# Dealing the first loads to three queues, and storing the last unit plainly: one change at both ends of a fused attention and Fourier-mix kernel

## The chip, the cores and the metric

The kernel runs on one core of a Trainium2 chip. A time is the device time of one launch in microseconds (us). The kernel before took 2325.61 us, the median of three runs (2323.56, 2325.61, 2325.95). A separate execution was recorded by the hardware profiler; its own time was 2316.28 us.

## The reference

All tensors are float32. The first half is talking-heads attention with 8 batches, 12 heads, 448 rows and head size 64; the second half is a Fourier mix followed by a feed-forward block.

```python
scores = (1 / sqrt(64)) * q @ k.T                       # per batch b and head h
scores = einsum('bhij,hg->bgij', scores, w_pre)         # mix heads before the softmax
attn = softmax(scores)                                  # over the last axis
attn = einsum('bhij,hg->bgij', attn, w_post)            # mix heads after it
x = (attn @ v), heads side by side                      # (8, 448, 768)
u = x + real(fft(fft(x, axis=1), axis=2))
un = (u - mean(u)) / sqrt(var(u) + 1e-6)
out = u + relu(un @ w_ch1) @ w_ch2                      # 768 -> 3072 -> 768
```

## The kernel before

The kernel has two phases. `mix_phase` does the attention and the Fourier mix; `ffn_phase` does the feed-forward block. The change touches the first 60 us of the one and the last 30 us of the other.

**The attention pipeline.** A batch has eight blocks of rows (`BLOCKS`), and a block has 2 or 3 *steps*, 23 in a batch, 184 in all. The data pass through these stages:

- `emit_load_qk` loads the rows of one head pair of q or k into a tile `raw`. A tile takes four DMAs (`y` is the half of the partitions, `x` the head), each of 112 KB. A batch has six such tiles, so 24 DMAs. `emit_load_v` loads v, six DMAs of 224 KB a batch.
- `emit_xpose` transposes a raw tile on TensorE (7 transposes, L598) and copies it out of PSUM in two parts, one on ScalarE and one on VectorE (`ENG`), into `qT` or `kT`.
- `emit_qk(n, xx)` computes the scores of block `n` for four heads (16 matmuls, L624) and copies them in two pieces into the score tile `Sb` (copies of every kind are on L487, the line of the helper `copy`). `ENG["QK"]` is "aa": both copies are on ScalarE. There are two `Sb` tiles, so the copies of block n wait until block n-2 has been read.
- `emit_gather(T)` rearranges the scores of step T, so that all heads of some rows lie on neighbouring partitions: four DMAs of 105 KB from `Sb` to a tile `Kr` (L641), on the queue of SyncE (SP).
- `emit_premix(T)` mixes heads (L652), `emit_max` takes row maxima on VectorE (L659), `emit_exp` exponentiates on ScalarE (L666), `emit_scale` normalises on GpSimd (POOL, L676), `emit_postmix` mixes heads again (L686), `emit_turn` transposes (L699).
- `emit_av` multiplies by v (L716); Fourier stages follow further on.

`emit_load_mix` loads the two small mixing matrices and a mask, seven small DMAs.

**The order** is written by hand. The main loop counts a step number `s` upward from the first entry. In each `s`, the gather is that of step s+5, the premix, maximum, exponential and scale are those of step s+2, and the postmix and turn are those of step s. All other work stands in four lists, filled by `due(kind, at, fn)`, and is issued when `s` reaches `at`. TensorE, VectorE, ScalarE and GpSimd keep exactly that order. A DMA issued from ScalarE or GpSimd therefore also stands in that engine's order: while the issue waits, what comes after it on the engine waits as well.

For the first batch all q and k loads are at -40 and in the order k, q for xx = 0, then 2, then 1 (`START`); of each pair of DMAs, `x = 0` is on SP and `x = 1` on ScalarE. The v loads follow on SP, then (-39) the seven small loads on SP. The six transposes are at -20 to -15, the scores of blocks 0 and 1 at -18 to -13 alternately. Block n from 2 on is at BLOCK_AT[n] - 8 + AT_QK[n][xx], which is -2, -1, 0 for block 2, then 1, 2, 2 for block 3 and 3, 4, 5 for block 4. The q and k of the second batch are loaded by GpSimd at the steps of `AT_L`: -4 and -3, -2 and -1, 0 and 1, 2 and 7, and so on.

**The last unit.** The feed-forward phase is cut into six chunks of the hidden dimension times seven tiles of 512 rows. A unit is one chunk of one tile: `first` computes the hidden part (L1208), `second2` the output part (L1330) as seven products j0, j3, j5, j6, j4, j1, j2, collected in tiles `od` by ScalarE (L1358) and VectorE (L1352). `both` adds one od tile to another (L1361). `out_` is a DMA from GpSimd that *adds* an od tile onto a quarter of the output tile in memory (L1364, 384 KB). `acc[t, r, d]` is the quarter with row half r and column half d. `on(s, ...)` places work at position s of the unit's 49 matmul pairs and their tail. In the last unit (`end`), two quarters, v12 and v22, are loaded from the output beforehand (`load`, L1338), the products are added to them on the chip, and they are written with two plain DMAs each, one on SP and one on ScalarE (`store`, L1368). The other two quarters are updated by four adding DMAs: j0 and j1 onto (0, 0), j3 and j6 onto (1, 0).

Of the kernel before, what the change touches and what calls it, by code (L numbers as in the profile page):

```python
# [17 lines left out]
B, NH, S, D = 8, 12, 448, 64  # L18
# [71 lines left out]
AT_L = ((-4, -3), (-2, -1), (0, 1), (2, 7), (10, 11), (12, 13))  # L90
AT_V = ((2, 3), (4, 5), (6, 7))
AT_QK = ((0, 2, 1), (0, 1, 2), (0, 1, 2), (1, 2, 2),
         (0, 1, 2), (0, 1, 2), (0, 1, 2), (0, 1, 2))
# [355 lines left out]
def mix_phase(ctx, tc, rest, ident, q, k, v, w_pre, w_post, u_scr, u_rev, wts, lead):  # L449
# [60 lines left out]
    def emit_load_mix():  # L510
        for t in dens:
            nc.gpsimd.memset(t[:, :, :], 1e-9)
        nc.gpsimd.memset(wrp[:, :, :], 0.0)
        nc.sync.dma_start(out=mk, in_=cn["mk"].ap())
        for x in range(2):
            for y in range(2):
                nc.sync.dma_start(
                    out=wrp[64 * x + 30 * y:64 * x + 30 * y + 30, 0, :],
                    in_=_ap(w_pre, 6 * y * NH, [[0, R], [NH, 6], [1, NH]]))
            nc.sync.dma_start(out=wrp[64 * x:64 * x + KR, 1, :],  # L520
                              in_=_ap(w_post, 0, [[0, R], [NH, NH], [1, NH]]))
# [33 lines left out]
    def emit_load_qk(b, xx, nm, y):  # L555

        src = q if nm == "q" else k
        if y == 0 and b == 0 and xx == START[-1]:

            if "raw" not in first:  # L560
                first["raw"] = ppv.tile([P, GT, 2 * S], F32, name="Pv", tag="Pv")
            batches[b]["raw" + nm, xx] = first["raw"][:, nm == "q"].rearrange(
                "p (c x d) -> p c x d", c=C7, x=2)
        elif y == 0:
            batches[b]["raw" + nm, xx] = praw.tile([P, C7, 2, D], F32, name="raw" + nm,
                                                   tag="raw")
        t = batches[b]["raw" + nm, xx]
        for x in range(2):
            eng = nc.gpsimd if b else (nc.sync, nc.scalar)[x]
            eng.dma_start(  # L570
                out=t[64 * y:64 * y + 64, :, x, :],
                in_=src[b, 6 * y + 2 * xx + x].rearrange("(p c) d -> p c d", c=C7))
        return True
# [10 lines left out]
    def emit_xpose(b, xx, nm):  # L584
# [6 lines left out]
        if nm == "q":  # L591
            nc.gpsimd.memset(t[:, :, 0:MG], 0.0)
            nc.gpsimd.memset(t[:, :, MG + S:WQ], 0.0)
        evs = []
# [15 lines left out]
    def emit_qk(n, xx):  # L610

        bk = blocks[n]
        st = batches[bk["b"]]
        if "Sb" not in bk:
            bk["Sb"] = psb.tile([P, 6, S], F32, name="Sb", tag="Sb")
# [3 lines left out]
        for y in range(2):  # L619
            for o in (64 * y, 64 * y + 32):  # L620
                lo = c0 + o - 64 + (0 if y else w)
                hi = min(lo + 32, c0 + w)
                for x in range(2):
# [4 lines left out]
                        start=True, stop=True)  # L628
        return [lambda x=x: copy(ENG["QK"][x], bk["Sb"][:n, 2 * xx + x, :],
                                 pss[x][:n, :S]) for x in range(2)]  # L630

    def emit_gather(T):

        Kr = pkr.tile([P, 2, S], F32, name="Kr", tag="Kr")
        n, j = at_step[T]
        Sb, rs = blocks[n]["Sb"], blocks[n]["rs"]
        row = _row(Sb)
        for z in range(2):
            for x in range(2):
                p0 = 64 - R * rs + 4 * j + 2 * z + x  # L640
                nc.sync.dma_start(  # L641
                    out=Kr[64 * x:64 * x + KR, z, :],
                    in_=_ap(Sb, p0 * row, [[rs * row, 2 * R], [S, 6], [1, S]]))
        steps[T]["Kr"] = Kr
# [242 lines left out]
    for b in range(B):  # L887
        f = b * GS
        at_t = [(a, nm, xx) for xx, at in enumerate(AT_T) for nm, a in zip("qk", at)]
        if b == 0:  # L890

            for i, xx in enumerate(START):
                for j, nm in enumerate("kq"):
                    for y in range(2):
                        due("none", -40, lambda xx=xx, nm=nm, y=y: emit_load_qk(0, xx, nm, y))
                    due("full", 2 * i + j - 20, lambda xx=xx, nm=nm: emit_xpose(0, xx, nm))
                for n in range(2):
                    due("QK", 2 * i + 2 + n - 20, lambda n=n, xx=xx: (emit_qk(n, xx), n))
            for pr in range(3):
                for y in range(2):  # L900
                    due("none", -40, lambda pr=pr, y=y: emit_load_v(0, pr, y))
        else:
            for at, (a, nm, xx) in zip(AT_L, sorted(at_t, key=lambda e: e[0])):
                for y in range(2):
                    due("none", f + at[y] - GS,
                        lambda b=b, xx=xx, nm=nm, y=y: emit_load_qk(b, xx, nm, y))
# [7 lines left out]
        for n in range(0 if b else 2, NBL):  # L914
            for xx in range(3):
                due("QK", f + BLOCK_AT[n] - 8 + AT_QK[n][xx],
                    lambda n=NBL * b + n, xx=xx: (emit_qk(n, xx), n))
# [24 lines left out]
    due("none", 0, lambda: wts.deal(0))  # L942
    due("none", -39, emit_load_mix)
    due("none", -3, emit_mix)
# [101 lines left out]
def ffn_phase(ctx, tc, rest, ident, u_scr, u_rev, wts, ub_scr, out, fold_rest,  # L1046
# [262 lines left out]
    def second2(n, st):  # L1309
# [76 lines left out]
        j0, j3, j5, j6, j4, j1, j2 = range(7)  # L1386
        v22, v12 = 7, 8
        pl = nc.gpsimd
# [5 lines left out]
        if end:  # L1394
            for v, r, d in ((v12, 0, 1), (v22, 1, 1)):
                on(0, load, v, r, d)
            on(24, out_, j0, 0, 0)
            on(27, out_, j3, 1, 0)
            for s, *o in ((33, vec, j5, j0), (34, pl, v12, j5), (41, vec, j6, j5),
                          (41, pl, v22, j6), (51.5, vec, v12, j4), (59, vec, v22, j4)):  # L1400
                on(s, both, *o)
            on(42, out_, j6, 1, 0)
            on(51.5, out_, j1, 0, 0)
            on(58, store, v12, 0, 1)
# [143 lines left out]
```

## Time and profile before

| | |
|---|---|
| median of three runs | 2325.61 us |
| profiled execution, its own time | 2316.28 us |
| its span, first to last instruction | 2314.3 us |
| TensorE busy | 2250.9 us, 97% of the span |
| VectorE, ScalarE, GpSimd busy | 1717.0, 1170.1, 1280.7 us |
| TensorE idle in the first 70 us | 24.3 us |
| last matmul to end of the span | about 11.6 us |

The profile names an instruction by its engine, its source line and the tiles it writes and reads ("Kr<-Sb"). "PEld" is the weight load, "SPq" or "ACTq" the queue of an engine that issues DMAs. In lists of instructions the first number is the start, the second the length, both in us, and the bracket at the end is the idle time before it and what ended that. In tables by stretch of time, each engine has its busy time and its count of instructions, and the last two columns are the mean busy share of the 16 DMA engines and what they moved.

### The profile page before, as it was taken

The numbers are of one execution on the slowest core, as the hardware profiler recorded it, in microseconds if no ns is written. First come the engines' busy times: TensorE is split into PE (matmuls) and PEld (weight loads), VectorE is DVE, ScalarE is ACT, GpSimd is POOL, SyncE is SP. The second block draws the span as 40 slices with busy tenths as digits, with TensorE's granted clock in tenths as the row PEclk, the third lists the DMA queues.
The fourth block names the chain that finished last, engine by engine and source line by source line (L and its number), as shares of the span: only waits on it lengthen the run. The fifth ranks groups of instructions, "written<-read, shape, count | busy, mean of one in ns | idle before, by whom it ended". The sixth has DMA issues, their size and how long they took to land.

```text
span 2314.3 us, 60776 instructions
## 1 busy us (share of the span) xinstructions
PE 2250.9 (97%) x22894; PEld 1737.6 (75%) x22894; DVE 1717.0 (74%) x3626; ACT 1170.1 (51%) x3336; POOL 1280.7 (55%) x1786
## 2 busy tenths in 40 slices
PE   5999999999999999999999999999999999999997
PEld 2545555555555577676899999999999999999997
DVE  2878888888878757777777787878778877765544
ACT  3776767666676632221345444444444445434433
POOL 3587868778787542221555454556555655453334
PEclk9999999999999999999999999999999999999999
DMA  7565665656656375668777887878787987796564
GB/s 164 160 185 163 190 175 163 193 160 190 181 175 196 133 260 190 209 200 290 216 171 192 227 228 187 220 182 247 207 190 186 278 193 174 186 257 124 133 144 75
DMA packets 232176, 439.44 MB, mean 190 GB/s; under 512 B 39624, under 2 KB 154336, under 8 KB 231886
## 3 DMA queue, kind: packets, MB, share of 16 engines
q1 hardware_dynamic: 157902, 302.97, 38.2%
q0 software_dynamic: 68128, 130.82, 29.9%
q8 instruction: 183, 3.00, 0.6%
q10 hardware_dynamic: 5856, 1.77, 0.4%
q14 instruction: 107, 0.88, 0.1%
HBM read 212.76 MB, written 143.55 MB: 154 GB/s over the span
## 4 chain that ended last, share of the span: by engine, by line
PE 85%; DVE 4%; DMA 3%; POOL 3%; ACT 2%; issue 1%; SPq 1%; ACTq 0%; DVEq 0%; POOLq 0%
PE psP L1208 17%; PE psP L1330 13%; PE psR L1208 9%; PE psR L1330 7%; PE mx L652 6%; PE ms L716 5%; PE ms L624 5%; PE psQ L1208 4%; PE po L686 4%; PE psQ L1330 3%; PE psP L1285 3%; DMA Kr<-Sb 2%; PE ms L841 2%; PE psR L1285 1%; PE ms L598 1%
## 5 line engine op out<-in xcount | busy, mean ns | idle before, releaser
L1364 POOL DMA_DIRECT2D out_dram<-od x174 | 211.4, 1281 | 260.2 <-DVE od L1352 179.8
L676 POOL TENSOR_SCALAR PP<-PP,rcp 128x448 f32<-128x448 f32 x368 | 235.9, 650 | 197.5 <-DVE rcp L674 154.5
L666 ACT ACTIVATE PP<-mx,nmx 128x448 f32<-128x448 f32 x368 | 230.2, 631 | 171.3 <-DVE nmx L659 156.0
L659 DVE TENSOR_REDUCE nmx<-mx 128x1 f32<-128x448 f32 x368 | 212.7, 618 | 95.7 <-PE mx L652 93.3
L1171 POOL TENSOR_TENSOR hq<-h 128x128 f32<-128x128 f32 (+1 forms) x210 | 129.8, 618 | 255.5 <-ACT h L1230 122.7
L1358 ACT COPY od<-psP 128x192 f32<-128x192 f32 x488 | 156.1, 320 | 170.7 <-PE psP L1330 169.3
L1361 DVE TENSOR_TENSOR od<-od 128x768 f32<-128x768 f32 x208 | 199.1, 971 | 51.8 <-ACT od L1358 51.7
L624 PE MATMUL ms<-kT,qT 64*32 64x448 f32 (+1 forms) x3072 | 199.3, 548 | 17.8 <-ACT Sb L487 7.5
L487 ACT COPY Sb<-ms 124x448 f32<-124x448 f32 (+1 forms) x384 | 184.6, 540 | 55.2 <-DMA Kr<-Sb 29.3
L699 DVE STREAM_TRANSPOSE Pv<-po 128x896 f32<-128x896 f32 x184 | 203.7, 1107 | 3.7 <-PE po L686 3.3
L652 PE MATMUL mx<-Kr,kw 60*32 60x448 f32 x2944 | 194.3, 548 | 8.5 <-ACT PP L666 4.6
L716 PEld LDWEIGHTS ms<-Pv,vv 64*64 64x64 f32 x5376 | 138.0, 132 | 70.3 <-issue 46.8
L686 PE MATMUL po<-PP,kw 60*32 60x448 f32 x2944 | 185.6, 537 | 1.6 <-POOL PP L676 1.1
L1208 PE MATMUL psP<-qs,w1t 128*128 128x256 f32 x744 | 179.2, 379 | 1.4 <-DVE h L1229 1.4
L1208 PE MATMUL psP<-ks,w1t 128*128 128x256 f32 x744 | 179.1, 379 | 0.1
L716 PE MATMUL ms<-Pv,vv 64*64 64x120 f32 (+1 forms) x5376 | 160.2, 263 | 1.3 <-ACT Sb L487 1.0
L252 POOL TENSOR_SCALAR wst<-wst 128x256 f32<-128x256 f32 (+1 forms) x76 | 118.2, 1563 | 68.9 <-ACT wst L263 67.6
L1208 PEld LDWEIGHTS psP<-qs,w1t 128*128 128x128 f32 x744 | 139.3, 190 | 18.3 <-DVE h L1229 1.8
L1208 PEld LDWEIGHTS psP<-ks,w1t 128*128 128x128 f32 x744 | 139.4, 190 | 16.7 <-DVE u L1290 0.7
L1208 PE MATMUL psP<-ub,w1t 128*128 128x256 f32 x528 | 127.1, 379 | 0.3 <-DVE h L1229 0.3
L624 PEld LDWEIGHTS ms<-kT,qT 64*32 64x32 f32 (+2 forms) x3072 | 56.0, 106 | 94.0 <-issue 58.3
L1229 DVE TENSOR_TENSOR h<-h,psP 128x512 f32<-128x512 f32 x42 | 28.8, 686 | 127.7 <-PE psP L1208 108.5
(190 smaller groups left out, 5354.2 us busy)
## 6 DMA issues: line engine op xcount, KB each, us to landing
Kr<-Sb SPq DMA_DIRECT2D x736, 105.0 KB
out_dram<-od POOLq DMA_DIRECT2D x174, 384.0 KB
qs<-ub SPq DMA_DIRECT2D x89, 384.0 KB
ks<-ub SPq DMA_DIRECT2D x88, 384.0 KB
ub<-ub SPq DMA_DIRECT2D x79, 384.0 KB
w1t<-w SPq DMA_DIRECT2D x42, 384.0 KB
w2t<-w SPq DMA_DIRECT2D x42, 384.0 KB
raw<-in_moe_w_ch_dram SPq DMA_DIRECT2D x32, 384.0 KB
```

What stands on the lines that cost most here:

```text
L624: nc.tensor.matmul(pss[x][o:o + hi - lo, :S], st["qT", xx][64 * x:64 * x + 64, y, lo:hi], st["kT", xx][64 * x:64 * x + 64, y, :], start=Tr ...
L652: nc.tensor.matmul(mx[x][64 * z + o:64 * z + o + 32, :S], kw1[64 * x:64 * x + KR, o:o + 32], Kr[64 * x:64 * x + KR, z, :], start=True, sto ...
L659: nc.vector.tensor_reduce(nmx[:, :], steps[T]["mx"][x][:, :S], axis=AX.X, op=ALU.max, negate=True)
L666: nc.scalar.activation(steps[T]["PP"][:, x, :], steps[T]["mx"][x][:, :S], ACTF.Exp, bias=steps[T]["nmx", x][:, :], accum_out=steps[T]["den ...
L676: nc.gpsimd.tensor_scalar(PP[:, x, :], PP[:, x, :], rcp[:, x:x + 1], 1.0, op0=ALU.mult, op1=ALU.mult)
L686: nc.tensor.matmul(po[o:o + 32, z, :S], kw2[64 * z:64 * z + KR, y, :], PP[64 * z:64 * z + KR, :, c * HS:(c + 1) * HS], start=True, stop=True)
L699: nc.vector.transpose(turned[a]["Pv"][:, j, :].rearrange("p (z s) -> p z s", z=2), steps[T]["po"][:, :, :S])
L716: nc.tensor.matmul(pss[y][64 * x:64 * x + 64, :nu * R], st["v", pr][64 * y:64 * y + 64, x, jb * D:(jb + 1) * D], _ap(Pv, 64 * y * rp + 32 ...
L1208: mm = nc.tensor.matmul(p[:, m, :], w1[i][:, kc, m * P:(m + 1) * P], ub[:, kc, :], start=i in (0, 4, 1)[:3 - seed] and m == kc == 0, stop= ...
L1330: nc.tensor.matmul(ps[j, key][:, :DQ], a, b, start=m in (0, 4), stop=True, skip_group_check=True)
L1361: eng.tensor_tensor(D[j][:, :, :], D[j][:, :, :], D[k][:, :, :], op=ALU.add)
L1364: nc.gpsimd.dma_start(out=acc[t, r, d], in_=D[j][:, :, :], accum_op=ALU.add)
```

## The change

At the start: the first batch's 24 loads of q and k are dealt 12 to SP, 4 to ScalarE (those of xx = 0) and 8 to GpSimd; the seven small loads go to GpSimd, ahead of them; the margins of the first three qT are cleared by VectorE. The score copies of blocks 0 and 1 are split between ScalarE and VectorE ("ad"). The scores of block 1 come after all of block 0 (-13, -12, -11), and those of blocks 2, 3 and 4 at 0, 1, 1, then 2, 3, 3, then 4, 5, 5. The gathers of steps 0, 1 and 2 are issued half from GpSimd. The second batch's first two tiles are loaded at -12, its third at 3 and 4, its fourth at 5 and 6.

In the last unit: a third quarter, v11, is loaded as well; j0 and j1 are added to it on VectorE (at 24 and 51.5) and it is written with plain DMAs at 52. j4 is added to v12 at 44, where it was 51.5. The adding DMA of j6 is issued straight after the sum j6+j5, ahead of GpSimd's v22+j6. The adding DMAs of j0 and j1 are gone.

```diff
+AT_L1 = ((-12, -12), (-12, -12), (3, 4), (5, 6), (10, 11), (12, 13))
+AT_QK0 = {2: (0, 1, 1), 3: (2, 3, 3), 4: (4, 5, 5)}
...
-        nc.sync.dma_start(out=mk, in_=cn["mk"].ap())
+        nc.gpsimd.dma_start(out=mk, in_=cn["mk"].ap())
         for x in range(2):
             for y in range(2):
-                nc.sync.dma_start(
+                nc.gpsimd.dma_start(
                     out=wrp[64 * x + 30 * y:64 * x + 30 * y + 30, 0, :],
...
-            nc.sync.dma_start(out=wrp[64 * x:64 * x + KR, 1, :],
+            nc.gpsimd.dma_start(out=wrp[64 * x:64 * x + KR, 1, :],
...
-            eng = nc.gpsimd if b else (nc.sync, nc.scalar)[x]
+            eng = nc.gpsimd if b else (nc.sync, nc.scalar if xx == START[0] else nc.gpsimd)[x]
...
-            nc.gpsimd.memset(t[:, :, 0:MG], 0.0)
-            nc.gpsimd.memset(t[:, :, MG + S:WQ], 0.0)
+            eng = nc.gpsimd if b else nc.vector
+            eng.memset(t[:, :, 0:MG], 0.0)
+            eng.memset(t[:, :, MG + S:WQ], 0.0)
...
+        engs = ENG["QK"] if n > 1 else "ad"
...
-        return [lambda x=x: copy(ENG["QK"][x], bk["Sb"][:n, 2 * xx + x, :],
+        return [lambda x=x: copy(engs[x], bk["Sb"][:n, 2 * xx + x, :],
...
-                nc.sync.dma_start(
+                (nc.gpsimd if x and T < 3 else nc.sync).dma_start(
                     out=Kr[64 * x:64 * x + KR, z, :],
...
-                for n in range(2):
-                    due("QK", 2 * i + 2 + n - 20, lambda n=n, xx=xx: (emit_qk(n, xx), n))
+                for n, at in enumerate((2 * i - 18, i - 13)):
+                    due("QK", at, lambda n=n, xx=xx: (emit_qk(n, xx), n))
...
-            for at, (a, nm, xx) in zip(AT_L, sorted(at_t, key=lambda e: e[0])):
+            for at, (a, nm, xx) in zip(AT_L if b > 1 else AT_L1, sorted(at_t, key=lambda e: e[0])):
                 for y in range(2):
-                    due("none", f + at[y] - GS,
+                    due("none", f + at[y] - GS if b > 1 else at[y],
...
-                due("QK", f + BLOCK_AT[n] - 8 + AT_QK[n][xx],
+                due("QK", AT_QK0[n][xx] if b == 0 and n in AT_QK0 else
+                    f + BLOCK_AT[n] - 8 + AT_QK[n][xx],
...
-    due("none", -39, emit_load_mix)
+    due("none", -41, emit_load_mix)
...
-        v22, v12 = 7, 8
+        v22, v12, v11 = range(7, 10)
...
         if end:
-            for v, r, d in ((v12, 0, 1), (v22, 1, 1)):
+            for v, r, d in ((v11, 0, 0), (v12, 0, 1), (v22, 1, 1)):
                 on(0, load, v, r, d)
-            on(24, out_, j0, 0, 0)
             on(27, out_, j3, 1, 0)
-            for s, *o in ((33, vec, j5, j0), (34, pl, v12, j5), (41, vec, j6, j5),
-                          (41, pl, v22, j6), (51.5, vec, v12, j4), (59, vec, v22, j4)):
+            on(41, both, vec, j6, j5)
+            on(41, out_, j6, 1, 0)
+            for s, *o in ((24, vec, v11, j0), (33, vec, j5, j0), (34, pl, v12, j5),
+                          (41, pl, v22, j6), (44, vec, v12, j4), (51.5, vec, v11, j1),
+                          (59, vec, v22, j4)):
                 on(s, both, *o)
-            on(42, out_, j6, 1, 0)
-            on(51.5, out_, j1, 0, 0)
+            on(52, store, v11, 0, 0)
             on(58, store, v12, 0, 1)
             on(60, store, v22, 1, 1)
```

## The prediction, made before the changed kernel was run

> **What bounds the kernel now.** I read the page's 40 slices first, then a table by stretch of time, then the timeline and the waits of the first 70 us, then the last 20 us. TensorE by slices:
>
> ```profile
> PE   5999999999999999999999999999999999999997
> ```
>
> TensorE is full everywhere but in the first and the last slice (58 us each), so only there can an edit of this kind buy anything. The table by stretch cuts the first slice up; the first number after the length is TensorE's busy time.
>
> ```profile
> core 0: us, PE busy (x) PEld busy (x) DVE busy (x) ACT busy (x) POOL busy (x), PEclk, DMA share, GB/s
> 15.00:29.00 14.00, 11.73 (x124) 4.99 (x124) 4.45 (x14) 7.43 (x16) 0.00 (x0) 1.00 0.89 162
> 29.00:43.00 14.00, 7.53 (x80) 2.28 (x88) 3.50 (x13) 4.77 (x13) 2.66 (x4) 0.88 0.37 130
> 43.00:58.00 15.00, 11.09 (x181) 5.28 (x176) 7.68 (x17) 8.15 (x22) 9.78 (x15) 0.89 0.66 190
> 58.00:70.00 12.00, 11.92 (x212) 5.33 (x202) 11.69 (x25) 8.85 (x23) 4.81 (x10) 1.00 0.42 142
> 70.00:90.00 20.00, 20.00 (x483) 10.50 (x468) 14.55 (x34) 14.66 (x49) 12.97 (x21) 1.00 0.49 156
> ```
>
> From 58 us on TensorE is the bound: whatever reaches that state earlier is kept. Of the first 58 us it is idle 24.2 us (11.6 in the 15 us before the first row, and 2.3, 6.5 and 3.9). The waits of this window and its timeline say why.
>
> ```profile
> ACT L487 <- DMA rawq<-in_q_dram: 12.4, 1, 12.4
> ACT Sb L487 <- DMA Kr<-Sb: 9.3, 2, 5.8
> ...
> 12.38 1.28 ACT L487 ACT_TABLE_LOAD   x1 [12.38 <-DMA rawq<-in_q_dram]
> ...
> 29.00 31.10 SPq L641 DMA_DIRECT2D Kr<-Sb  x35
> ...
> 53.75 0.97 ACT L487 COPY Sb<-ms 124x448 f32<-124x448 f32 x2 [5.84 <-DMA Kr<-Sb]
> ```
>
> First, ScalarE issues twelve loads, each waiting for room, and starts its first copy only at 12.38 + 1.28 = 13.7; so the first scores start at 15.05, though q was transposed by 9.7. Second, block 0 is complete at 29.0, where the gathers start, one per 0.81 us on one queue. Third, ScalarE stands in front of score copies that wait for the gathers of block n-2, 3.4 us at 40.5 and 5.8 us at 53.75, with exponentials queued behind. Step 0 is scaled at 37.67 and step 8 at 69.60, 4.0 us a step, where undisturbed steps (60.64, 63.41, 66.04) take 2.7.
>
> At the other end, TensorE and VectorE finish but DMAs do not:
>
> ```profile
> 2302.15 2.46 POOL L1364 DMA_DIRECT2D out_dram<-od  x2 [1.04 <-DVE od L1352]
> ...
> 2307.00:2308.00 1.00, 0.00 (x0) 0.00 (x0) 0.00 (x0) 0.00 (x0) 0.00 (x0) 0.52 1.13 326
> 2310.00:2311.00 1.00, 0.00 (x0) 0.00 (x0) 0.00 (x0) 0.00 (x0) 0.00 (x0) 0.50 0.74 169
> ```
>
> VectorE ends at 2304.8. From 2304 to 2311 the engines move four transfers of 384 KB: two adding ones, issued at 2302.15, and two plain ones. The span ends 3.5 us later.
>
> **What the Trainium skill says.** "DMA: Bandwidth & Descriptors", section "Issuing engines are not separate DMA queues": DMAs of all issuers share the same 16 engines, so a second issuer saves only issue time. The trace agrees: about 200 GB/s from 5 to 19 us, with two queues or three. The same page, "Queues, rings and completion order": each engine goes round the queues packet by packet. From 13 to 19 us the three queues moved 0.31, 0.31 and 0.46 MB, near equal thirds, GpSimd's the largest. "TensorE: Matmul & The Clock Gate", Part 1: after idling, the array runs at half clock for some 3.4 us. Seven transposes take 1.73 us here until 20 us, then 0.98. "GPSIMD Engine Reference", section 1: GpSimd shares its memory interface with VectorE instructions that have two SBUF inputs. The od sums take 0.96 us on VectorE, and 1.47 beside GpSimd's.
>
> **The change, part by part.**
>
> *Scalar queue freed.* ScalarE issues 4 loads of about 0.6 us and is free at about 3.5; its table load (1.28) hides before the first transposes (5.8 to 7.5). q of xx = 0 is in PSUM at 9.7 and copied by 10.6, so block 0's first scores start there and not at 15.05. From then I count, with the rows of before: scores 1.74, two transposes 1.73 and 1.3, copy 0.9, scores 1.0, two transposes 2.0, copy 1.0, scores 1.0, halved copy 0.6. Sum 11.3, so block 0 is complete at about 21.9, against 29.0. Taking block 1's scores out of this chain (1.74, 1.24 and their copies) is in that. Bounds 20 (TensorE warm early) and 24 (cold throughout).
>
> *Data.* GpSimd first issues seven small loads (0.57 each, as its two loads of 'rows' take 1.15), so until about 6, then 8 loads at 0.72, until 12. 24 loads are 2.75 MB, v is 1.38, the second batch's first two tiles, now both early, 0.92: 5.05 MB. The 4.80 MB of before (0.67 of the second batch) took from 2.6 to 25.6, 209 GB/s; so 24.2 us, until 26.8. The gathers stand behind v on SP's queue and behind the second batch's tiles on GpSimd's, so issuing them at 21.9 doesn't land them: step 0's 0.43 MB (2.1 us) is there at about 28.9. **The DMAs, not ScalarE, become the bound**, and the first premix, 31.6 now, comes at 28.9. This costs part of the gain of the freed queue. The last q tile, at equal shares, lands by 16.7, before its turn at about 17.
>
> *Gathers on two queues.* 12 gathers at 0.81 took 9.7 us on SP; six take 4.9 there, six about the same on GpSimd (0.6 to 1.0 each, the small loads and the q loads as bounds), which has nothing else to do then. Both are over at about 27. Steps 1 and 2 need as much each: there at 31.0 and 33.1, against 40.4 for step 2. SP goes on with steps 3 to 5, 12 x 0.8 to about 36, against 48.7.
>
> *Scores of blocks 2, 3, 4 later.* Block 2's copies come behind the exponentials of steps 0 and 1, at about 37, when step 2's gather (33.1) has long landed: the stall of 3.4 goes. Block 3's come at step 2, about 43, when step 5's has landed (38): the 5.8 goes. What is late next is block 4 at step 4, about 48, waiting for step 7's gather, about 48.5. Moving them also puts them nearer to their own gathers, at step 1 (block 2) and 3 (block 3): SP waits there, which costs nothing as long as a gather (3.2 and 2.6 landing) fits the three steps until its premix.
>
> *Sum of the start.* Step 0 is fully gathered at 28.9, premixed 0.95, scaled 3.3 later (34.3 to 37.67): 33.1, against 37.67. At 2.8 us a step, step 8 is scaled at 55.5, against 69.6: 14.1 us. I take off 2.1 for remaining stalls and a cold array: **12 us**, bounds 5 (only the earlier start) and 16. From there the order is as before and TensorE the cover.
>
> *VectorE's margins and halved copies.* Six memsets of 0.1 us and copies of 0.55 on an engine that has 4.5 of 14 us busy: nothing. On GpSimd they would stand behind the loads.
>
> *The second batch's third and fourth tiles later.* Needed at step 13 and 15, loaded at 3 to 6: seven steps of cover, nothing.
>
> *Last unit.* v11's load joins v12's and v22's, more than 35 us before the end, and takes the ninth od buffer; v22 then takes the slot of the unit before, free at about 2280. VectorE adds v11+j0 (0.96) in its idle 1.34 at 2292.9: nothing. At 44 it now adds v12+j4, 0.96 to 1.47, just before the last PSUM collections; TensorE waits for those, so 0.4 to 0.9 us is lost. The sum v11+j1 takes the place of the one moved. GpSimd issues j6's DMA at 2299.3 or when j3's has landed; j3's now has no j0 beside it. Its bytes go by before 2303.5. What is left at the end is three plain stores, 1.18 MB, from about 2305.4 at 330 GB/s, 3.6 us: 2309, against 2310.8. **1.8 us gained**, bounds 0 and 3.
>
> Together 12 + 1.8 = 13.8 us. On the profiled execution that is 2316.3 - 13.8 = 2302.5; the median of runs stands 9.3 us above the profiled one, so 2311.8, rounded to 2312. Less than 0.2%, 4.7 us, counts as no change.
>
> **Rivals.**
>
> *A, the forecast, 0.66:* both stalls go, 13.8 us.
>
> *B, the backlog stays in front, 0.15:* the early tiles and v hold the gathers until 30 or more, block 3 still stalls, and only the start's 5 plus 1.5 at the end remain: 2319. For it: DMAs busy 9 tenths until 25.6 already. Against: a gap of 3 us before the first gather now.
>
> *C, swallowed, 0.11:* the steps that come early meet another limit, as at 124 us, where a gather takes 6.1 us to land and ScalarE waits 4.3 in an ordinary batch. Two such waits more: about 2323.
>
> *D, slower, 0.08:* GpSimd's queue becomes the bound. It issues 7 + 8 + 8 + 6 = 29 DMAs ahead of step 0's scale, in order. At 0.7 each they end at 22. Step 8 is level with before if step 0 is scaled at 69.6 - 22.4 = 47.2, that is at 1.57 us each; at 1.8 the run is some 5 us slower, 2331. Against: the dearest DMA on GpSimd here takes 1.2 (384 KB, adding).
>
> **How the numbers follow.** The range runs from 2305 (16 + 3 gained, and 1.5 for the spread of runs) to 2322 (B and a part of C). Faster: A, and B nearly whole, 0.8. Within 0.2%: C and the rest of B, 0.12. Slower: D, 0.08.
>
> **What would show it.** Right: ScalarE's table load before 5 us; gathers from about 22; step 0's scale at 31 to 34, step 8's at 53 to 58; no wait of score copies on gathers over 2 us before step 8; at the end no adding DMA after 2304 minus the shift, and the last bytes some 4 us after VectorE's end. Wrong: GpSimd's DMAs spaced over 1 us, the first premix after 31, or TensorE idle over 20 us in the first 58.

## The result, and the profile after

In the runs that compare the two kernels on one chip, 22 each, the changed kernel took 2312.59 us (2307.86 to 2319.48) and the kernel before 2318.39 us (2311.62 to 2326.91). The ratio is **0.9973, 95% interval 0.9962 to 0.9985**: faster, by about 6 us. The forecast of 2312 us lies on the measured time, but partly by luck: it counted 13.8 us off a time near the median of 2325.61, and that kernel's median is 7 us lower in these runs. The gain itself is less than half of the forecast, and the forecast's range, 2305 to 2322 us, would have held the kernel before in these runs too.

The one profiled execution after is longer than the one before (span 2317.0 us against 2314.3), although the runs are shorter. The code that no edit touches explains that: from the scale of step 18 to that of the last step, 183, it took 687.6 us before, 693.7 after, and 685.5 to 696.0 in the twelve other kernels of this study, which have the same code there. So the profiles are used for the first 110 us and the last 20, and the timed runs for the sum.

TensorE in 40 slices, from the page of the kernel after:

```profile
PE   7999999999999999999999999999999999999998
```

The first slice went from 5 to 7, the last from 7 to 8. The table by stretch of the kernel after, with the columns of the one before:

```profile
15.00:29.00 14.00, 9.15 (x100) 4.25 (x98) 7.84 (x26) 4.92 (x8) 6.55 (x11) 1.00 1.07 204
29.00:43.00 14.00, 11.24 (x105) 3.48 (x113) 5.99 (x14) 4.89 (x14) 3.19 (x6) 0.63 0.58 179
43.00:58.00 15.00, 14.49 (x256) 7.07 (x246) 11.06 (x23) 11.49 (x32) 10.30 (x17) 1.00 0.44 116
58.00:70.00 12.00, 10.05 (x168) 5.07 (x155) 7.67 (x14) 6.61 (x16) 4.60 (x9) 1.00 0.73 192
70.00:90.00 20.00, 20.00 (x509) 10.86 (x509) 14.92 (x35) 14.53 (x53) 13.05 (x21) 1.00 0.44 140
```

TensorE's idle time in the first 58 us fell from 24.2 to 16.0 us. Two rows show why that is not a gain of 8 us. From 29 to 43 us TensorE is busy 11.24 us, 3.7 more than before, but with 105 matmuls in place of 80, at a mean clock of 0.63: part of that busy time is slow matmuls. From 58 to 70 us, where it had been busy for 11.92 of 12 us, it now idles for 2 us. The lines of the timeline of the kernel after that answer to those shown of the kernel before, with the scales of steps 0, 8 and 9:

```profile
3.44 1.28 ACT L489 ACT_TABLE_LOAD   x1 [3.44 <-issue]
...
25.09 3.36 POOL L645 DMA_DIRECT2D Kr<-Sb  x6 [3.52 <-ACT Sb L489]
...
35.27 1.26 POOL L680 TENSOR_SCALAR PP<-PP,rcp 128x448 f32<-128x448 f32 x2 [6.81 <-DVE rcp L678]
...
64.12 1.25 POOL L680 TENSOR_SCALAR PP<-PP,rcp 128x448 f32<-128x448 f32 x2 [1.75 <-DVE rcp L678]
...
68.08 0.97 ACT L489 COPY Sb<-ms 124x448 f32<-124x448 f32 x2 [4.60 <-DMA Kr<-Sb]
...
70.92 1.27 POOL L680 TENSOR_SCALAR PP<-PP,rcp 128x448 f32<-128x448 f32 x2 [5.55 <-DVE rcp L678]
```

ScalarE is free at 3.4, and the two old waits of score copies for gathers, 3.4 us for block 2 and 5.8 us for block 3, are gone. But two new ones stand behind them, 1.9 us at 56.4 (block 4) and 4.6 us at 68.08 (block 5), and step 9, late for it, is scaled at 70.9. The scale times tell the start step by step (us, from the traces):

| step scaled | 0 | 2 | 5 | 8 | 9 | 18 |
|---|---|---|---|---|---|---|
| before | 37.7 | 46.6 | 60.6 | 69.6 | 73.0 | 108.7 |
| after | 35.3 | 42.9 | 51.7 | 64.1 | 70.9 | 106.4 |
| gained | 2.4 | 3.7 | 8.9 | 5.5 | 2.1 | 2.3 |
| forecast | 4.6 | | | 14.1 | | 12 |

Nine microseconds are gained by step 5 and seven of them are gone by step 9. From there on nothing changes: from step 9 to step 18 it takes 35.7 us before and 35.5 after, and TensorE is busy for 98 to 99% of that time in both. Step 18 therefore tells what a start is worth:

```profile
108.68 1.26 POOL L676 TENSOR_SCALAR PP<-PP,rcp 128x448 f32<-128x448 f32 x2 [2.08 <-DVE rcp L674]
```

```profile
106.44 1.26 POOL L680 TENSOR_SCALAR PP<-PP,rcp 128x448 f32<-128x448 f32 x2 [2.25 <-DVE rcp L678]
```

Kernels of this study with the same start differ by about 1 us at step 18: before and e2 give 108.7 and 110.7, mean 109.7; after, e1 and e4 give 106.4, 108.0 and 107.2, mean 107.2. So the start is worth **2.5 us**, not 12.

The waits of SP's queue in the first 66 us of the kernel after (us in total, times, longest) show where the 9 us went:

```profile
SPq L645 <- DVE Sb L489: 10.0, 1, 10.0
SPq L645 <- ACT Sb L489: 7.0, 2, 6.4
```

The first is the wait before the very first gather. The second is new: SP has issued step 5's last gather at 39.9 us and then waits 6.4 us for block 2's score copies, which now stand at steps 0 and 1. The timeline of SP's queue from 44 us on, kernel after, shows the gathers of step 6 starting:

```profile
46.40 1.57 SPq L645 DMA_DIRECT2D Kr<-Sb  x2
```

and that from 50 us on shows that SP then issues without a break:

```profile
49.70 20.77 SPq L645 DMA_DIRECT2D Kr<-Sb  x24
```

Before, step 6's gathers started at 48.7: of 9 us only 2.3 is left at this point, and whatever depends on step 6 and later starts from there.

The end, first two lines of the kernel before (the last `psQ` copy and VectorE's last sum), then the kernel after:

```profile
2299.03 0.30 ACT L1349 COPY psQ<-psP 128x192 f32<-128x192 f32 x1 [0.33 <-PE psP L1330]
...
2303.82 0.95 DVE L1361 TENSOR_TENSOR od<-od 128x768 f32<-128x768 f32 x1
```

```profile
2305.32 0.30 ACT L1354 COPY psQ<-psP 128x192 f32<-128x192 f32 x1 [0.33 <-PE psP L1335]
...
2307.17 1.20 POOL L1369 DMA_DIRECT2D out_dram<-od  x1 [2.54 <-issue]
...
2307.95 2.27 POOL L1366 TENSOR_TENSOR od<-od 128x768 f32<-128x768 f32 x1
...
2308.47 0.56 PE L1335 MATMUL psP<-w2t,hq 128*128 128x192 f32 x2 [1.24 <-DVE od L1357]
...
2311.07 1.73 SPq L1373 DMA_DIRECT2D out_dram<-od  x3
...
2311.50 0.94 DVE L1366 TENSOR_TENSOR od<-od 128x768 f32<-128x768 f32 x1
```

The last adding DMA is issued at 2307.17 (j6); its bytes go by until 2312.5, and those of the plain stores behind it, from 2311.9 to 2315.6. I measure from the last `psQ` copy, which both kernels have: to VectorE's end 5.74 us before and 7.12 after; from there to the end of the span 9.57 and 4.60. Over the kernels of this study with the new end the sum is 11.0 to 12.0 us (mean 11.4), over the three with the old end 13.9 to 15.3 (mean 14.5): about **3.1 us gained** (g3 below, whose last unit is different again, is left out). With the start's 2.5 that is 5.6 us; the runs say 6 (3.5 to 8.8).

### The profile page after: what moved, and what is told of

Same layout as the page of the kernel before. It is cut to its first block, busy times and chain, and to the rows that moved or that the text cites. A ratio compares the mean times of both kernels' runs of the same rounds, so it can differ in the third digit from the quotient of the medians.

```text
span 2317.0 us, 60784 instructions
## 1 busy us (share of the span) xinstructions
PE 2260.0 (98%) x22894; PEld 1743.0 (75%) x22894; DVE 1719.4 (74%) x3640; ACT 1167.7 (50%) x3330; POOL 1292.1 (56%) x1799
## 4 chain that ended last, share of the span: by engine, by line
PE 88%; DVE 5%; DMA 3%; ACT 2%; issue 1%; POOL 1%; SPq 1%; DVEq 0%; ACTq 0%; POOLq 0%
PE psP L1213 18%; PE psP L1335 14%; PE psR L1213 9%; PE psR L1335 7%; PE mx L656 6%; PE ms L720 6%; PE ms L628 5%; PE po L690 5%; PE psQ L1213 4%; PE psQ L1335 3%; PE psP L1290 3%; PE ms L845 2%; PE ms L601 2%; DMA Kr<-Sb 1%; PE psR L1290 1%; PE ms L829 1%
## 5 line engine op out<-in xcount | busy, mean ns | idle before, releaser
L656 PE MATMUL mx<-Kr,kw 60*32 60x448 f32 x2944 | 199.0, 555 | 7.4 <-DMA Kr<-Sb 4.2
L720 PEld LDWEIGHTS ms<-Pv,vv 64*64 64x64 f32 x5376 | 137.9, 132 | 76.7 <-issue 46.4
L1234 DVE TENSOR_TENSOR h<-h,psP 128x512 f32<-128x512 f32 x42 | 28.8, 686 | 127.8 <-PE psP L1213 112.3
L1335 PE MATMUL psP<-w2t,hq 128*128 128x192 f32 x490 | 122.4, 332 | 1.2 <-DVE od L1357 1.2
```

The source lines that it names most:

```text
L656: nc.tensor.matmul(mx[x][64 * z + o:64 * z + o + 32, :S], kw1[64 * x:64 * x + KR, o:o + 32], Kr[64 * x:64 * x + KR, z, :], start=True, sto ...
L720: nc.tensor.matmul(pss[y][64 * x:64 * x + 64, :nu * R], st["v", pr][64 * y:64 * y + 64, x, jb * D:(jb + 1) * D], _ap(Pv, 64 * y * rp + 32 ...
L1335: nc.tensor.matmul(ps[j, key][:, :DQ], a, b, start=m in (0, 4), stop=True, skip_group_check=True)
```

## The experiments

"Step 18" is the time at which step 18 is scaled; ratios are to the kernel before, run beside it on the same chip, with 95% intervals, so two experiments are compared through their ratios. The landing of a gather is the last count of its semaphore in the trace. The theory going in was that the moved scores of blocks 2 to 4 hold SP back and so waste the freed ScalarE; the rivals were that the DMA backlog in front of the gathers does it, or the second batch's tiles.

**e1 and e2: each end of the change alone.** e1 is the kernel after with the old last unit, e2 the kernel before with the new one.

```diff
...
-            on(41, out_, j6, 1, 0)
...
-            on(52, store, v11, 0, 0)
+            on(42, out_, j6, 1, 0)
+            on(51.5, out_, j1, 0, 0)
...
```

> The start of the changed kernel with the last unit of the kernel before. The changed kernel's profile scales step 18 at 106.4 us, the kernel before at 108.7, so I read the start as worth 2.3 us of the 5.8 measured. Theory 'two halves': faster than before by about 2.3 us (0.1%), step 18 at 106.4, and a tail of 9.5 us from VectorE's end to the span's end as before. Rival 'start as forecast': the start is worth 8 to 12 us and the profiles hide it by a later loss; then 2306 to 2310 where before is 2318.

> The last unit of the changed kernel with the start of the kernel before. Theory 'two halves': faster than before by about 3.6 us (0.15%): VectorE ends 1.4 us later against TensorE's work and the tail after it is 4.6 instead of 9.5 us. Rival 'end as forecast': 1.8 us, with a tail of 7 us or more. Step 18 stays at 108.7.

Measured: e1 0.9999 (0.9986 to 1.0012), e2 0.9985 (0.9969 to 1.0). The start alone can't be told from no change, though its trace repeats that of after (step 8 at 64.3, step 18 at 108.0); the end alone brings some 3.5 us (0 to 7), in line with its trace (11.40 us from the last `psQ` copy to the end of the span). As far as intervals of this width allow, more than half of what the change gains comes from the end, where the forecast had put an eighth of it.

**e3: scores of blocks 2, 3, 4 back to their old places.**

```diff
-AT_QK0 = {2: (0, 1, 1), 3: (2, 3, 3), 4: (4, 5, 5)}
+AT_QK0 = {}
```

> The changed kernel with the scores of blocks 2, 3 and 4 back at their places of before (-2, -1, 0; 1, 2, 2; 3, 4, 5). Theory 'gap on SP': in the changed kernel SP stands idle from 39.9 to 46.4 us, since block 2's scores come so late that step 6 can't be gathered, and at 0.81 us a gather it never catches up. Then here step 6's gathers start at 40 to 43 instead of 46.4, ScalarE waits no more than 1.5 us for gathers (the gathers of block 0 land by 34.4, the first exponentials end at 34.6), and step 18 is scaled at 102 to 104 instead of 106.4. Rival 'the later scores help, as the change intends': the waits of ScalarE come back (3 us or more at block 2 and 5 at block 3), and step 18 is at 108 or later.

Measured: **0.9942 (0.9921 to 0.9962)**, 2306.22 us, some 7 us below the kernel after by the two ratios. Step 5 is at 49.2, step 8 at 59.5, step 18 at 101.2. The waits of SP's queue in the first 66 us, e3:

```profile
SPq L645 <- DVE Sb L489: 10.4, 1, 10.4
...
SPq L645 <- ACT Sb L489: 0.4, 1, 0.4
```

and the stretches of e3 by engine:

```profile
29.00:43.00 14.00, 12.13 (x172) 4.82 (x177) 9.83 (x32) 8.44 (x23) 4.34 (x8) 0.88 0.60 182
```

The 6.4 us wait is gone, step 6's gathers start at 41.0 in place of 46.4, and TensorE does 172 matmuls from 29 to 43 us where after did 105. One line of the change, meant to spare ScalarE a stall, costs 6 us at step 18. In the old places the two stalls do not return in their old size, because the gathers that they waited for now come earlier: the copies of block 2 wait 0.58 us, until 34.7, where it had been 3.4, and those of block 3 wait 0.72 us, where it had been 5.8. The longest wait before 75 us is 3.9, just before step 9; that ScalarE would wait no more than 1.5 us did not come true. The lines of step 18:

```profile
101.17 1.26 POOL L680 TENSOR_SCALAR PP<-PP,rcp 128x448 f32<-128x448 f32 x2 [2.08 <-DVE rcp L678]
```

**e4: the v loads behind the first gathers.** Six v loads moved from -40 to step 1.

```diff
-                    due("none", -40, lambda pr=pr, y=y: emit_load_v(0, pr, y))
+                    due("none", 1, lambda pr=pr, y=y: emit_load_v(0, pr, y))
```

> The changed kernel with the six loads of v of the first batch at step 1 on SP, where its queue is idle, instead of ahead of the first gathers. Theory 'backlog': the first gathers were issued at 24.5 and landed at 29.1 to 34.4, as 5.05 MB lay in front of them, and TensorE went to half clock meanwhile. Without v's 1.38 MB they land at 27 to 30, step 0 is scaled at 31 to 33 instead of 35.3, steps 1 and 2 follow at 3 us instead of 3.3 and 4.4, and step 6's gathers start 4 to 6 us earlier; step 18 at 101 to 104. Rival 'gap on SP alone': step 0 comes earlier, but the gathers of step 6 on stay behind their scores and v takes SP's time and the DMA engines' there; step 18 within 1 us of 106.4.

Measured: 0.9987 (0.9974 to 1.0), step 18 at 107.2. It tests nothing: the trace shows the v loads still issued from 9.75 to 14.4 us. The kernel fixes the order of TensorE, VectorE, ScalarE and GpSimd alone, and SP's does not follow the place in the list. So e4 counts as a repeat of the whole kernel after, and its ratio, a gain of 3 us (0 to 6), lies below the 6 us (3.5 to 8.8) of the first comparison.

**f1: e3, and the second batch's third and fourth tiles at 8 to 10.**

```diff
-AT_L1 = ((-12, -12), (-12, -12), (3, 4), (5, 6), (10, 11), (12, 13))
+AT_L1 = ((-12, -12), (-12, -12), (8, 9), (9, 10), (10, 11), (12, 13))
```

> The changed kernel with the scores of blocks 2 to 4 at their places of before, as in e3, and in addition the third and fourth tile of the second batch loaded at 8 to 10 instead of 3 to 6. In e3 these loads run from 47.7 to 59 us, the gathers then take 4 to 5.8 us to land instead of 2.3, and ScalarE waits 3.9 us for them before step 9 (59.5 to 65.5). Theory 'the loads hold up the gathers': gathers issued at 50 to 60 us land in 2.3 to 3 us, ScalarE's longest wait for a gather in the first 75 us is under 2 us, step 18 is scaled at 98 to 99.5 instead of 101.2. Rival 'SP's issue rate alone': the same wait within 1 us and step 18 at 100.5 to 102.

Measured: 0.9961 (0.9947 to 0.9975). Step 9 is at 62.1 where e3 has 65.5, but step 18, expected at 98 to 99.5, at 104.7 where e3 has 101.2. ScalarE's waits for gathers before 75 us, f1 and then e3:

```profile
ACT Sb L489 <- DMA Kr<-Sb: 2.8, 3, 1.4
```

```profile
ACT Sb L489 <- DMA Kr<-Sb: 6.9, 4, 3.9
```

and f1's table by stretch after that:

```profile
58.00:70.00 12.00, 12.00 (x279) 6.63 (x279) 8.93 (x23) 7.83 (x27) 8.08 (x13) 1.00 0.47 149
70.00:90.00 20.00, 15.95 (x367) 8.54 (x352) 11.46 (x27) 11.58 (x39) 14.27 (x22) 0.92 0.81 187
```

So the wait before step 9, 3.9 us in e3, is for the most part these loads': step 10's last gather, for which the copies of block 5 wait, is issued at 56.6 in e3 and takes 5.7 us to land, and at 56.2 in f1 and takes 2.7. In the kernel after (4.6 us) that gather takes 5.7 us too. But the bytes have to go by at some time. In f1 they meet the gathers of later steps, and TensorE idles 4 us between 70 and 90.

**f2 and f3: e3 with less in front of the first gathers.** f2 issues v from GpSimd at -2, f3 loads the second batch's first two tiles at 0 to 2.

```diff
-        (nc.gpsimd if b else nc.sync).dma_start(
+        nc.gpsimd.dma_start(
...
-                    due("none", -40, lambda pr=pr, y=y: emit_load_v(0, pr, y))
+                    due("none", -2, lambda pr=pr, y=y: emit_load_v(0, pr, y))
```

```diff
-AT_L1 = ((-12, -12), (-12, -12), (3, 4), (5, 6), (10, 11), (12, 13))
+AT_L1 = ((0, 1), (1, 2), (3, 4), (5, 6), (10, 11), (12, 13))
```

> As e3, and the first batch's v loaded from GpSimd at -2, after the three split gathers, instead of from SP at the beginning (e4 didn't move them: SP's order isn't written by hand, and they were still issued ahead of the gathers). Theory 'backlog': 1.38 MB less lies in front of the first gathers, which land at 27 to 30 instead of 28.5 to 34; step 0 is scaled at 31 to 32.5 instead of 34.7, and step 18 comes 1 to 3 us earlier than e3's 101.2. Rival 'queue only': step 0 comes earlier, but v now collides with the gathers of steps 3 to 7 and step 18 is at 101 or later.

> As e3, and the first two tiles of the second batch loaded at 0 to 2 instead of -12, 0.92 MB less in front of the first gathers. Theory 'backlog': the gathers on GpSimd, which stand behind these tiles, land at 27.5 to 30 instead of 30.2 to 33.4; step 0 is scaled 1 to 3 us earlier than 34.7. After that the loads run beside the gathers of steps 5 to 8, so step 18 is at 100 to 102.5. Rival 'v's loads are the whole backlog': step 0 within 0.7 us of 34.7, and step 18 later than 101.5.

Measured: f2 0.9976 (0.9964 to 0.9988), f3 0.9959 (0.9946 to 0.9972). Step 0 comes at 32.15 and 31.92 us, 2.5 and 2.8 before e3's: the backlog is what holds the first gathers, as the rival says. But step 8 stands at 64.0 and 62.9, against 59.5, and step 18 at 104.1 and 102.2, against 101.2. What is taken from the front comes back behind it. In f2 it shows as one wait of ScalarE:

```profile
ACT Sb L489 <- DMA vv<-in_v_dram: 5.5, 1, 5.5
```

The view names v, but a score copy does not read v. It waits for the gathers of block 0, some of which share their semaphores with loads of v, and the last of these gathers, issued at 28.8, lands at 36.93, when the wait ends: 8.1 us beside v's bytes, where a gather alone takes 2.4.

**f4: the kernel after, all gathers on SP.** One run.

```diff
-                (nc.gpsimd if x and T < 3 else nc.sync).dma_start(
+                nc.sync.dma_start(
```

> The changed kernel with the gathers of steps 0 to 2 all on SP, as before. Theory 'gap on SP': SP issues steps 0 to 5 in 24 x 0.81 us from 24.5, to 44, and the gap before step 6 (at 46.4 in the changed kernel) shrinks from 6.5 to 3 us or less, so step 6's gathers start within 2 us of where they did and step 18 is within 1.5 us of 106.4. Rival 'the split gathers carry the gain of the start': step 18 at 109 or later.

Measured: 2316.86 us, which says nothing beside a spread of 12 us. The trace says more. Counted from the first gather's issue, the four gathers of steps 0, 1 and 2 have all landed after 6.6, 8.4 and 11.5 us here on one queue, and after 7.0, 9.1 and 10.0 us in the kernel after on two (30.2, 32.0, 35.1 us and 31.5, 33.5, 34.5 us). The second queue issues sooner what then waits for the same engines: it brings the third step forward, and the two that are needed first come a little later. SP's break before step 6 shrinks from 6.5 us to 2.6, as expected, but step 6's gathers still start at 46.0: block 2's scores set that time, not the length of the break. Step 18 is at 104.5, earlier than the 106.4 to 108.0 of the three kernels with the split and 1.9 from the 106.4 that was expected within 1.5.

**g1: e3, with the second batch's tiles spread over the steps.**

```diff
-AT_L1 = ((-12, -12), (-12, -12), (3, 4), (5, 6), (10, 11), (12, 13))
+AT_L1 = ((-12, -12), (0, 2), (4, 6), (8, 9), (10, 11), (12, 13))
```

> As e3 (scores of blocks 2 to 4 at their places of before), with the second batch's six tiles spread: the first at -12, then 0 and 2, 4 and 6, 8 and 9, 10 and 11, 12 and 13. f1 took the collision at step 9 away (step 9 at 62.1 instead of 65.5) and met a new one at steps 10 to 18, as eight loads came in three steps; f3 brought step 0 to 31.9 and lost it at steps 5 to 8. Theory 'crowding': one load of two DMAs every second step costs less than either; step 0 at 33 to 34, step 9 at 61 to 63, step 18 at 98.5 to 100.5. Rival 'the bytes decide, not their places': step 18 within 1.5 us of e3's 101.2.

Measured: 0.9947 (0.9931 to 0.9964), 2303.80 us, step 18 at 101.8. It can't be told from e3, and step 9 comes at 64.8, not at the 61 to 63 expected: this spreading decides little.

**g2: the dealing alone.** The kernel before with the loads dealt to three queues, the small loads on GpSimd and the margins on VectorE.

```diff
...
-            eng = nc.gpsimd if b else (nc.sync, nc.scalar)[x]
+            eng = nc.gpsimd if b else (nc.sync, nc.scalar if xx == START[0] else nc.gpsimd)[x]
...
-    due("none", -39, emit_load_mix)
+    due("none", -41, emit_load_mix)
```

> The kernel before with nothing but the dealing of the first loads (12, 8, 4, the small loads ahead on GpSimd, the margins on VectorE). ScalarE's first copy then comes at about 7.5 instead of 13.7. Theory 'the queue of ScalarE bounded the first scores': block 0 is complete at 25 to 27 instead of 29.0 (block 1's scores still lie between), step 0 is scaled at 34 to 36 instead of 37.7, and step 18, with the waits for gathers as before, at 105 to 108 instead of 109.7 (the mean of the two profiles with that start). Rival 'the dealing alone buys nothing, the order of the scores does': step 0 at 37 or later, step 18 at 109 or later.

Measured: 0.9979 (0.9961 to 0.9997), step 18 at 104.1, 5.6 us before the mean of 109.7:

```profile
104.06 1.27 POOL L677 TENSOR_SCALAR PP<-PP,rcp 128x448 f32<-128x448 f32 x2 [2.09 <-DVE rcp L675]
```

Step 0 (33.7) and step 18 come even before the times expected. By the traces this one edit gains at the start twice what the whole start of the change does; by its ratio 5 us, with an interval from 1 to 9.

**g3: e3, with v12+j4 on GpSimd,** to take it out of VectorE's way, and j6's DMA behind it.

```diff
-            on(41, out_, j6, 1, 0)
...
-                          (41, pl, v22, j6), (44, vec, v12, j4), (51.5, vec, v11, j1),
+                          (41, pl, v22, j6), (44, pl, v12, j4), (51.5, vec, v11, j1),
...
+            on(44, out_, j6, 1, 0)
```

> As e3, and in the last unit the sum v12+j4 on GpSimd instead of VectorE, after v22+j6, and j6's adding DMA behind both. In the changed kernel VectorE's v12+j4 delays the last PSUM collections, TensorE waits 1.24 us for them, and VectorE ends 7.1 us after the last psQ copy instead of 5.7; GpSimd stands 2.5 us before j6's DMA. Theory 'VectorE's added sum costs 1.4 us': VectorE ends 5.7 to 6.2 us after that copy, and the span ends 0.5 to 1.2 us earlier against it. Rival 'the bytes bound the end': VectorE ends earlier, but j6's adding DMA now lies beside the plain stores and the span ends no earlier, or later.

Measured: 0.997 (0.996 to 0.9981), some 6 us above e3 by the two ratios. The start is that of e3 (step 18 at 101.2); from the last `psQ` copy to VectorE's end it takes 9.22 us, against 6.91 in e3, and to the end of the span 13.64, against 11.09. The end thus explains 2.6 of the 6 us. The rest has no place in the traces, and the intervals of the two ratios leave 1 to 12 us, so 2.6 alone may be all of it. The end's timeline, g3:

```profile
2300.03 3.57 POOL L1366 TENSOR_TENSOR od<-od 128x768 f32<-128x768 f32 x2 [0.89 <-DVE od L1366]
...
2303.64 0.35 DVE L1357 TENSOR_TENSOR od<-od,psR 128x192 f32<-128x192 f32 x1 [3.42 <-POOL od L1366]
2303.91 0.61 DVE L1357 TENSOR_TENSOR od<-od,psP 128x192 f32<-128x192 f32 x2
...
2304.67 0.94 PE L1335 MATMUL psP<-w2t,hq 128*128 128x192 f32 x2 [2.92 <-DVE od L1357]
```

The theory fell: the sum is not hidden on GpSimd. Its two sums take 3.57 us, VectorE's next collection waits 3.42 us for them, and TensorE, in turn, 2.92 us for VectorE. The sum at 44 has a collection waiting behind it.

**g4: e3 without two more edits,** the split of the gathers and the early tiles.

```diff
-AT_L1 = ((-12, -12), (-12, -12), (3, 4), (5, 6), (10, 11), (12, 13))
+AT_L1 = AT_L
...
-                (nc.gpsimd if x and T < 3 else nc.sync).dma_start(
+                nc.sync.dma_start(
...
-                    due("none", f + at[y] - GS if b > 1 else at[y],
+                    due("none", f + at[y] - GS,
```

> As e3, without two more edits: all gathers on SP, and the second batch's tiles loaded at their places of before. What is left of the start is the dealing, block 1's scores after block 0's, and the halved copies. f4 lost nothing by putting the gathers on SP. Theory 'dealing and order carry the start': step 0 at 32 to 35, step 18 within 1.5 us of e3's 101.2, time within 3 us of e3's. Rival 'the early tiles and the split gathers are part of it': step 18 at 104 or later.

Measured: 0.9971 (0.9956 to 0.9985), step 0 at 32.9 but step 18 at 103.2, between what theory and rival expected. The two edits together are worth 2 us at step 18 in e3. As f4 gives the split nothing, it would be the early tiles that are worth it, but f4 has the later scores, and neither edit was tried alone in e3.

## Why the prediction was right, and where its size was wrong

The direction and the range held. Of 13.8 us, about 6 came, 3 in the repeat e4. Of the signs it named for being right, the table load (3.4 us) and the waits before step 8 (1.9 us) came true; the first gathers (24.5, not 22), step 0 and step 8 did not. None of its signs for being wrong came: GpSimd's DMAs, the first premix at 29.3 us, and TensorE's 16.0 us of idling are all within their bounds.

- **Scalar queue freed: right in kind, 2.6 us off.** The table load is at 3.44, and both early stalls are gone. Block 0 is complete at 24.5, not 21.9 and just past the bound of 24: the transposes of q for xx = 1 wait until 20.6 us for data, which the forecast had landing by 16.7. GpSimd's loads did take 0.72 us each.
- **Data: the bound was named rightly, its end was off.** The loads land until about 29.6, not 26.8. Step 0's gather, due whole at 28.9, is whole at 31.5. The first premix starts at 29.32, near the 28.9 forecast, but with four matmuls, and waits for the rest; step 0 is scaled at 35.3, not 33.1, and outside the window of 31 to 34.
- **Gathers on two queues: the issue was right, the landing was not.** GpSimd's are 0.54 to 0.60 us apart, and both queues' first twelve are issued by 29.6. But steps 1 and 2 are there at 33.5 and 34.5, not at 31.0 and 33.1, and f4 shows that one queue brings steps 0 and 1 no later and only step 2 later. "DMA: Bandwidth & Descriptors" in the Trainium skill says under "Issuing engines are not separate DMA queues" that several issuers only save the time of issuing; f4 agrees (7.0 us to step 0 on two queues, 6.6 on one). The forecast quoted it and still let the split save time.
- **Scores of blocks 2, 3, 4 later: the step that failed.** It said: "SP waits there, which costs nothing as long as a gather (3.2 and 2.6 landing) fits the three steps until its premix". A step needs four gathers, and SP issues one in 0.81 us: 3.25 us a step, where a step takes 2.8 us in the forecast and 2.9 in e3 from step 0 to 5. So SP, ahead at 39.9 us, was itself close to the bound, and 6.4 us of idling can't be made up before step 9: the premixes of steps 6 and 7 start piece by piece as their gathers land. The forecast checked one gather's latency against its deadline and not the queue's rate against the step. e3 shows the price: 6 us at step 18, 7 us in the time. That the rate is the reason is read from SP's unbroken issuing, and was not tested by itself.
- **The second batch's third and fourth tiles later: "nothing" was wrong.** The forecast looked at when they are needed and not at what they run beside. Issued from 50 to 62 us, they stretch the landing of a gather from 2.4 to over 5 us, and ScalarE waits 4.6 us at 68.08, a stall of the kind that the change took away at 53.75. f1 shows, in e3's order, that most of the stall is theirs, and also that moving them later moves it.
- **Sum of the start.** It said 14.1 us at step 8 less 2.1. Step 8 came at 64.1, not 55.5: 2.2 of the 8.6 us were there at step 0; steps 0 to 5 took 16.4 us in place of 14.0 (2.4), steps 5 to 8 took 12.4 in place of 8.4 (4.0). Then 3.4 more went at step 9. The 2.1 us "for remaining stalls and a cold array" had to cover all of it.
- **Last unit: right, too small.** On the mean of the kernels with each end, the tail after VectorE shrank by 4.3 us (5.0 in the pair before and after), and VectorE's own end moved back by 1.2, for which the forecast had 0.4 to 0.9: 3.1 us, not 1.8, and just above the bound of 3. The bytes came out about as forecast: the last ones go by 3.0 us after VectorE's end where it had been 6.2, a net gain of 2.0. What the forecast put at nothing is the stretch from the last byte to the end of the span, 2.1 to 3.2 us with adding DMAs among the last and 1.3 to 2.0 with plain stores alone: 1.1 us more. Why it shrinks was not tested. The adding DMA of j6 was later than forecast; its bytes end at 2312.5, as VectorE does.

Of the rivals, D is out (GpSimd's small loads, loads and gathers take 0.55 to 0.78 us, not 1.57; the 1.2 us held against D as the dearest DMA of GpSimd was misread, since adding DMAs take up to 1.7 us in the kernel before). B had half the mechanism and nearly the size, 6.5 us: the backlog does stay in front until 29.6, but block 3 does not stall. C, two new waits of some 4 us, is close to what happened, with SP's wait as one of them, though it had neither of the places.

The stretch from step 9 to 18 takes 35.4 to 37.1 us in every kernel of this study but f1, with TensorE busy for 98 or 99% of it, so TensorE is the bound there, as the forecast had it from 58 us on; only f1, with 42.6 us and 4.2 of them idle, loses there. What stays open is the stretch before it: f2, f3 and g4 gain at step 0 on e3 and lose more than that up to step 9, and what bounds this stretch as a whole was not found. Nor can the edits' shares be added up beyond this: 5.6 us for the dealing, some 3 for the rest of the start, 6 back for the later scores, each with about 1 us of spread.

**The better version** is e3 (0.9942) or g1 (0.9947): the change as it is, without its table of later scores. Both beat the kernel before and, by the ratios, the kernel after; they rest on six and nine runs.

## What to carry to other kernels

When work is moved later because its consumer seems to have time, compare the consumer's *rate* with the step, not only the latency of one transfer with its deadline: a queue that needs 3.25 us for a step of 2.8 has no idle time to give. When several edits attack the same stall, try the last one without the others: here the dealing had already brought the gathers forward, and the cure for the stall had become the stall. Bytes that are moved off one gather's path land on another's, so a load's "cover" must name what it runs beside.

## What the runs showed of the hardware

**A cold array can be as dear as the stall that cooled it.** The premixes of steps 1, 2 and 3 in the timeline of the kernel after, each of 16 matmuls:

```profile
34.12 2.33 PE L656 MATMUL mx<-Kr,kw 60*32 60x448 f32 x16 [0.88 <-ACT PP L670]
37.40 2.33 PE L656 MATMUL mx<-Kr,kw 60*32 60x448 f32 x16 [0.95 <-ACT PP L670]
41.50 1.23 PE L656 MATMUL mx<-Kr,kw 60*32 60x448 f32 x16
```

"TensorE: Matmul & The Clock Gate", Part 1, tells of the half clock after idling; here the recorded clock is at half from 30.9 to 41.1 us, though TensorE idles for no more than 0.95 us at a time in it. That is three times the 3.4 us for which the forecast quoted the page. In the four kernels with the later scores the mean clock from 29 to 43 us is 0.54 to 0.63; in those with e3's order it is 0.88 to 1.00, except f2, where gathers land late beside v (0.68). The page puts the ramp under 1% of a typical span. That holds, but two premixes at 1.1 us each are about as much as this whole start gained.

**A small transfer pays for its neighbours.** A gather of 105 KB lands 2.4 us after its issue when alone. In the kernel after it takes 4.9 to 5.8 us beside the second batch's loads (issued at 55.4 to 67.0 us), and 5.2 to 5.9 us when GpSimd issues it beside the first backlog; in e3 it takes up to 7.3.
